# Attention and a rational layer on one core: top bits of early weights on GpSimd, and keys instead of masks

## The chip, the core and the metric

The program runs on one core of one Trainium2 chip, in one launch. The metric is the device time in microseconds from start to end; three runs of a kernel are made and their median stands for it. Times within a run come from one profiled execution.

## What is computed

Queries, keys and values have 4 batches, 8 heads, 768 positions and 64 columns. Each chunk of 32 queries looks at a window of 16 keys to its left, its own 32, 8 to its right, and 8 memory keys. At the ends of a sequence the window is cut. The result goes through a layer with a rational function between two products.

```python
for c in range(nc):                                   # chunks of 32 queries
    l_start, r_end = max(0, c_start - 16), min(S, c_end + 8)
    k_full = np.concatenate([mem_k, k[:, :, l_start:r_end]], axis=2)
    v_full = np.concatenate([mem_v, v[:, :, l_start:r_end]], axis=2)
    scores = scale * np.matmul(q_c, k_full.transpose(0, 1, 3, 2))
    a = np.exp(scores - np.max(scores, axis=-1, keepdims=True))
    a = a / (np.sum(a, axis=-1, keepdims=True) + 1e-09)
    out[:, :, c_start:c_end] = np.matmul(a, v_full)
...
h = x @ w_in                                          # x: 3072 x 512, w_in: 512 x 2048
P = a[0] + a[1] * h + a[2] * h2 + a[3] * h3
Q = 1.0 + np.abs(b[0]) * np.abs(h) + np.abs(b[1]) * h2
return (P / (Q + 1e-6)) @ w_out                       # w_out: 2048 x 512
```

The weights w_in and w_out are 64-bit floats. The kernel gets them as 64-bit integers and makes 32-bit floats of them itself.

## The kernel before

**Tiles.** The 3072 rows are eight blocks of 384. For each block there are four units of attention (two heads each), which fill x of that block, and 16 steps of the layer, one for each 128 columns of w_in: `g1` makes h (12 matmuls, line 462), a chain on ScalarE, GpSimd and VectorE makes the rational function, and `g2` adds to the block's three outputs (9 matmuls, line 477). Both x and the weights are split into a high and a low part for TensorE (x_hi, x_lo, w_hl), so each product is three.

**Attention of a unit.** Scores go to PSUM (line 347). On VectorE a memset puts -1e30 on the scores of absent keys (lines 357 and 359; 307 and 309 for blocks from the fourth on), a reduction finds the maximum (362), a subtraction makes e (365). ScalarE takes the exponential (369), TensorE transposes (384), ScalarE copies (391), TensorE multiplies with v, which has a column of ones for the sum (402); VectorE divides (412 to 415, making xt), TensorE transposes back (425), ScalarE makes x_hi and xf (429, 432), GpSimd or VectorE x_lo (438, 442). A block is one half of a batch's sequence, so each unit has one chunk at an end of the sequence, the left one in even blocks and the right one in odd, and its memset covers the keys that are absent there.

**Weights.** A weight tile j has two halves, "in" and "out", of 128 x 512 words each, 64 bits a word. The order of the 32 halves is i0 o0 i1 o1 i4 i2 i3 o3 and so on. A half passes five steps, which the code's letters name: w (SP issues the load into w_raw), A (`w_abs`: ScalarE brings the high word's exponent to the range of 32 bits, line 172, into a PSUM tile stage), B (`w_bits`: VectorE shifts stage left by 3, line 177, then joins it with the top three bits of the low word, line 178, in place of that low word), H (ScalarE rounds to w_hl, line 185) and L (GpSimd subtracts to get the low part, line 190). The raw buffer is loaded anew when all its steps are done.

**The chain of the layer.** For each step: ScalarE ha and cy (513, 514), GpSimd cy (518), ScalarE ct (523), VectorE ct (527, 528), ScalarE cr by a logarithm and an exponential (532, 533), VectorE 537 to 539, GpSimd ghi and glo (544, 551).

**What sets the order.** The start, up to the 30th step, is a string of such letters written out by hand (SEQ). Every instruction is pinned in that order, and each engine works its own in that order; an instruction that waits holds up all behind it on its engine. A letter issues all its instructions together, whatever the engine. Loads are all issued by SP, in order. Later steps follow a fixed loop.

Of the kernel before, what the change touches and what calls it, by code (L numbers as in the profile page):

```python
# [16 lines left out]
ALU = mybir.AluOpType  # L17
AX = mybir.AxisListType

CHUNK = 32  # L20
LEFT = 16
RIGHT = 8
WIN = LEFT + CHUNK + RIGHT
MEM = 8
NEG = -1e30
F64_REBIAS = 2.0 ** -111
SIGN_STEP = 2.0 ** 32
W_SCALE = 2.0 ** 8
# [29 lines left out]
"""  # L58
QK_SLOTS = {0: [12, 13, 14, 15], 1: [12, 13, 14, 15], 2: [15, 16]}
WHOLE = 13  # L60
LAST = 122
FINAL = """
o g s p i j t r u y  o g s p i j t r u y  g s p i j t r u y o  g s p i j t r u y  g s p i j t r u y o  s p i j t r u y  o o u y o o
# [10 lines left out]
def attn_moe(ctx, tc, qk, vm, w, ab, out):  # L74
    nc = tc.nc
    P = 128
# [5 lines left out]
    NG = TB // P  # L82
    KEYS = P // 2
# [36 lines left out]
    def pin(ins):  # L120
        if pinned[0]:
            tc.keep_in_program_order(ins)
# [7 lines left out]
    conv, raws, split = {}, {}, {}  # L130
# [28 lines left out]
    def words(key):  # L159
        t = half(raws[key[1]], key[0]).rearrange("p (f two) -> p f two", two=2)  # L160
        return t[:, :, 0], t[:, :, 1]
# [6 lines left out]

    def w_abs(key):
        low, high = words(key)  # L170
        f = conv[key] = ps_a.tile([P, DM], F32, name="stage", tag="pa")
        pin(nc.scalar.activation(f, high.bitcast(F32), AF.Prelu, scale=F64_REBIAS, alpha=-SIGN_STEP))

    def w_bits(key):
        low, high = words(key)
        fi = conv.pop(key).bitcast(U32)
        pin(nc.vector.tensor_scalar(fi, fi, 3, None, op0=ALU.logical_shift_left))  # L177
        pin(nc.vector.scalar_tensor_tensor(low, low, 29, fi, op0=ALU.logical_shift_right, op1=ALU.bitwise_or))

# [123 lines left out]
    def pair_max(i, p):  # L303
        u = unit[i, p]
        sv = u.pop("s")
        if i % 2 == 0:
            pin(nc.vector.memset(sv[0:CHUNK, :, 0, 0:LEFT], NEG))
        else:
            pin(nc.vector.memset(sv[P - CHUNK:P, :, NG - 1, KEYS - RIGHT:KEYS], NEG))
        mx = sm.tile([P, 2, NG], F32, name="mx")  # L310
        pin(nc.vector.tensor_reduce(mx, sv, axis=AX.X, op=ALU.max))
        e = u["e"] = at.tile([P, NG, KEYS, 2], F32, name="e", tag="e", bufs=2)
        turned = e.rearrange("x g w h -> x g (w h)").rearrange("x g (b h k) -> x g b h k", b=4, h=2)
        for h in range(2):
            pin(nc.vector.tensor_tensor(turned[:, :, :, h], sv[:, h].rearrange("x g (b k) -> x g b k", b=4),
                                        mx[:, h].unsqueeze(2).unsqueeze(3).broadcast_to([P, NG, 4, KEYS // 4]), op=ALU.subtract))
# [33 lines left out]
    def att_max(i, p):  # L350
# [2 lines left out]
        u = unit[i, p]  # L353
        s = u.pop("s")
        sv = s[:, :NG * 2 * KEYS].rearrange("x (g h w) -> x g h w", g=NG, h=2)
        if i % 2 == 0:
            pin(nc.vector.memset(sv[0:CHUNK, 0, :, 0:LEFT], NEG))
        else:
            pin(nc.vector.memset(sv[P - CHUNK:P, NG - 1, :, KEYS - RIGHT:KEYS], NEG))
        mx = sm.tile([P, NG * 2], F32, name="mx")  # L360
        s3 = s[:, :NG * 2 * KEYS].rearrange("x (n w) -> x n w", w=KEYS)
        pin(nc.vector.tensor_reduce(mx, s3, axis=AX.X, op=ALU.max))
# [191 lines left out]
    done = dict.fromkeys("wABHL", 0)  # L554
# [146 lines left out]
    evac(*order[-1])  # L701


def padded(x, mem):
    x = np.pad(x, ((0, 0), (0, 0), (LEFT, RIGHT), (0, 0)))
    return np.concatenate([x, mem], axis=2)


def spread(first, count, S):
# [8 lines left out]
def lay_out(q, k, v, mem_k, mem_v):  # L718
    B, H, S, D = q.shape
    n = S // CHUNK // 2  # L720
    kp, vp = padded(k, mem_k), padded(v, mem_v)
    spans = [spread(half * n, n, S) for half in range(2)]
    keys = WIN + MEM
    kt = np.stack([kp[:, :, rows] for rows in spans], axis=2)
# [3 lines left out]
    qk = np.stack([np.concatenate([kt[:, :, 0], qt[:, :, 0]], axis=3),  # L728
                   np.concatenate([qt[:, :, 1], kt[:, :, 1]], axis=3)], axis=2)
    qk[BLOCKWISE:, :, 1] = np.concatenate([kt[BLOCKWISE:, :, 1], qt[BLOCKWISE:, :, 1]], axis=3)  # L730
    vw = np.concatenate([vw, np.ones(vw.shape[:4] + (1,), vw.dtype)], axis=4)
    vm = vw.reshape(B, H // 2, 2, 2, n, keys, D + 1).transpose(0, 3, 1, 2, 5, 4, 6)
    vm = np.array(vm.reshape(2 * B, H // 2, 2, keys, n * (D + 1)))
    late = vm[BLOCKWISE:].reshape(2 * B - BLOCKWISE, H // 2, 2, 4, keys // 4, n * (D + 1))
# [20 lines left out]
```

## Time and profile before

| | |
|---|---|
| median of three runs | 619.96 us (619.09 to 620.35) |
| the profiled execution | 619.44 us |
| its span, first to last instruction | 617.6 us |
| TensorE, matmuls | 599.1 us, 97% |
| VectorE | 495.3 us, 80% |
| ScalarE | 435.8 us, 71% |
| GpSimd | 433.0 us, 70% |

The span is what the instructions take; 1.84 us of the profiled execution lie around it. Shares of the whole span hide that the kernel has two parts: a start, in which loads, weights and attention are made ready, and a long row of matmuls. The start has to be read in order of time, engine by engine: a row shows when an instruction began, how long it took and, in brackets, how long the engine stood idle before it and what ended that.

### The profile page before, as it was taken

What the parts mean: (1) busy time and instruction counts of PE and PEld (TensorE: products, weight loads), DVE (VectorE), ACT (ScalarE), POOL (GpSimd) and SP (SyncE); (2) the same over time, 40 slices, a digit from 0 to 9 for tenths busy, and PEclk for the clock granted to TensorE, in tenths of its full rate; (3) what the DMA queues carried; (4) which work ended last, traced back from release to release, by engine and by line L of the source; (5) the groups of instructions that cost most, each with busy time, mean ns of one, the idle gap of its engine ahead of it and who ended that gap; (6) DMA issues with size and microseconds to landing.
All of it is one profiled execution on the core that took longest, in us unless ns stands there. A gap on an engine that the chain in (4) does not pass through costs nothing.

```text
span 617.6 us, 14151 instructions
## 1 busy us (share of the span) xinstructions
PE 599.1 (97%) x5275; PEld 528.8 (86%) x5275; DVE 495.3 (80%) x991; ACT 435.8 (71%) x822; POOL 433.0 (70%) x459
## 2 busy tenths in 40 slices
PE   6689999999999999999999999999999999999997
PEld 5568889899888888988889898888889888989996
DVE  6899998898867979788778787777878777666674
ACT  5799888798756766666667766676676766676674
POOL 2579987879966667766767676766767676776773
PEclk9999999999999999999999999999999999999999
DMA  7989437103023574342221322242122310010001
GB/s 259 359 280 360 162 110 254 48 1 146 2 83 86 177 212 146 119 133 81 82 81 38 116 68 75 81 133 82 36 62 68 101 27 14 14 51 2 0 1 51
DMA packets 42788, 64.81 MB, mean 105 GB/s; under 512 B 25696, under 2 KB 25696, under 8 KB 42336
## 3 DMA queue, kind: packets, MB, share of 16 engines
q1 hardware_dynamic: 41856, 60.61, 30.6%
q10 hardware_dynamic: 576, 1.74, 0.9%
q0 software_dynamic: 288, 1.57, 0.8%
q8 instruction: 41, 0.67, 0.4%
q14 instruction: 27, 0.22, 0.1%
HBM read 46.60 MB, written 9.44 MB: 91 GB/s over the span
## 4 chain that ended last, share of the span: by engine, by line
PE 53%; issue 18%; POOL 15%; DMA 5%; DVE 4%; ACT 2%; SPq 1%; POOLq 0%; DVEq 0%
PE o L477 25%; PE h L462 24%; POOL glo L551 6%; POOL ghi L544 6%; DMA qk<-in_qk_dram 2%; DMA w_raw<-in_w_dram 2%; POOL x_lo L440 1%; PE pairs L300 1%; POOL cy L518 1%; PE pairs L323 1%; SPq L125 1%; DMA v_main<-in_vm_dram 1%; DVE stage L177 1%; PE pa L347 1%; DVE ct L528 1%
## 5 line engine op out<-in xcount | busy, mean ns | idle before, releaser
L462 PE MATMUL h<-x_hi,w_hl 128*128 128x384 f32 x1024 | 265.1, 339 | 0.9 <-DVE ct L528 0.5
L477 PE MATMUL o<-w_hl,ghi 128*128 128x512 f32 x768 | 239.6, 393 | 0.0
L518 POOL TENSOR_TENSOR cy<-cy,ha 128x384 f32<-128x384 f32 x128 | 130.4, 1019 | 140.8 <-ACT cy L514 135.5
L462 PEld LDWEIGHTS h<-x_hi,w_hl 128*128 128x128 f32 x1024 | 185.3, 188 | 12.6 <-DVE ct L528 2.1
L462 PE MATMUL h<-x_lo,w_hl 128*128 128x384 f32 x512 | 172.5, 337 | 0.0
L477 PEld LDWEIGHTS o<-w_hl,ghi 128*128 128x128 f32 x768 | 141.8, 188 | 20.8 <-issue 0.8
L477 PE MATMUL o<-w_hl,glo 128*128 128x512 f32 x384 | 150.9, 393 | 0.0
L551 POOL TENSOR_TENSOR glo<-ct,ghi 128x384 fp32r<-128x384 f32 x127 | 129.1, 1017 | 8.9
L513 ACT ACTIVATE ha<-h 128x384 f32<-128x384 f32 x128 | 62.9, 492 | 91.7 <-PE h L462 89.4
L527 DVE TENSOR_TENSOR ct<-ct,h 128x384 f32<-128x384 f32 x128 | 70.1, 548 | 57.6 <-ACT ct L523 57.4
L544 POOL TENSOR_TENSOR ghi<-ct,zero 128x384 fp32r<-128x384 f32 x127 | 105.4, 830 | 3.8 <-DVE ct L539 2.7
L537 DVE SCALAR_TENSOR_TENSOR ct<-ct,par,cr 128x384 f32<-128x384 f32 x128 | 78.5, 613 | 33.9 <-ACT cr L533 30.9
L532 ACT ACTIVATE cr<-cy 128x384 f32<-128x384 f32 x128 | 63.2, 494 | 58.3 <-POOL cy L518 54.1
L462 PEld LDWEIGHTS h<-x_lo,w_hl 128*128 128x128 f32 x512 | 96.0, 188 | 0.0
L514 ACT ACTIVATE cy<-ha,bab 128x384 f32<-128x384 f32 x128 | 90.9, 710 | 4.5 <-DVE cr L538 0.3
L477 PEld LDWEIGHTS o<-w_hl,glo 128*128 128x128 f32 x384 | 72.0, 187 | 20.2 <-POOL glo L551 0.8
L523 ACT ACTIVATE ct<-h,par 128x384 f32<-128x384 f32 x128 | 84.1, 657 | 0.1
L528 DVE SCALAR_TENSOR_TENSOR ct<-ct,par,h 128x384 f32<-128x384 f32 x128 | 78.7, 615 | 4.5
L539 DVE SCALAR_TENSOR_TENSOR ct<-cr,ct 128x384 f32<-128x384 f32 x128 | 71.4, 558 | 4.4
L538 DVE SCALAR_TENSOR_TENSOR cr<-cy,cr 128x384 f32<-128x384 f32 x128 | 71.1, 556 | 0.4
L533 ACT ACTIVATE cr<-cr 128x384 f32<-128x384 f32 x128 | 60.8, 475 | 4.0
L190 POOL TENSOR_TENSOR w_hl<-w_raw,w_hl 128x512 fp32r<-128x512 f32 x32 | 42.1, 1316 | 6.8 <-ACT w_hl L185 6.1
(69 smaller groups left out, 406.9 us busy)
## 6 DMA issues: line engine op xcount, KB each, us to landing
w_raw<-in_w_dram SPq DMA_DIRECT2D x26, 512.0 KB, 7.0
v_main<-in_vm_dram SPq DMA_DIRECT2D x20, 390.0 KB, 4.7
qk_pairs<-in_qk_dram SPq DMA_DIRECT2D x16, 424.0 KB, 4.2
out_dram<-stage SPq DMA_DIRECT2D x24, 256.0 KB, 3.8
qk<-in_qk_dram SPq DMA_DIRECT2D x24, 212.0 KB, 4.8
v_main<-in_vm_dram SPq DMA_DIRECT2D x20, 195.0 KB, 6.0
eT<-blocks SPq DMA_DIRECT2D x80, 48.0 KB, 2.0
xf<-blocks SPq DMA_DIRECT2D x80, 48.0 KB, 2.0
```

The costliest lines, as they stand in the source:

```text
L462: pin(nc.tensor.matmul(h[:, :TB], lhsT=wt[:, cols], rhs=xt[i][:, ct, :], start=m == 0, stop=m == last))
L477: ins = nc.tensor.matmul(o, lhsT=gt[:, cols], rhs=wt, start=begin and m == 0, stop=end and m == 2)
L514: pin(nc.scalar.activation(c["y"], c["ha"], AF.Identity, scale=B1, bias=B0))
L518: pin(nc.gpsimd.tensor_tensor(c["y"], c["y"], c.pop("ha"), op=ALU.mult))
L523: pin(nc.scalar.activation(c["t"], c["h"], AF.Identity, scale=A3, bias=A2))
L527: pin(nc.vector.tensor_tensor(t, t, h, op=ALU.mult))
L528: pin(nc.vector.scalar_tensor_tensor(t, t, A1, h, op0=ALU.add, op1=ALU.mult))
L537: pin(nc.vector.scalar_tensor_tensor(t, t, A0, r, op0=ALU.add, op1=ALU.mult))
L538: pin(nc.vector.scalar_tensor_tensor(r, yy, QC, r, op0=ALU.add, op1=ALU.mult))
L539: pin(nc.vector.scalar_tensor_tensor(t, r, 2.0, t, op0=ALU.subtract, op1=ALU.mult, reverse0=True))
L544: pin(nc.gpsimd.tensor_tensor(ghi, chain[z]["t"], zero.broadcast_to([P, TB]), op=ALU.add))
L551: pin(engine.tensor_tensor(glo, chain.pop(z)["t"], gh[z].bitcast(F32), op=ALU.subtract))
```

## The change

It has two parts. For the first eight halves of weights, `w_abs` gets an instruction on GpSimd that reads the upper 16 bits of each low word, multiplies by 2 to the power -13, caps at 7 and writes that over the low word: the word's top three bits. VectorE then needs one instruction where it had two: it shifts stage left by 3 and joins it with that word. The other 24 halves stay as they were.

The memsets on scores are gone in all units. Instead, where a key is absent, the host's layout has a copy of the first memory key, and v has a row of zeros there, its column of ones too. The maximum over a row is then the same, and an absent key adds nothing to the sum or to the product.

```diff
+TOP_BITS = 8
...
     def w_abs(key):
         low, high = words(key)
+        if done["A"] < TOP_BITS:
+            tops = half(raws[key[1]], key[0]).bitcast(mybir.dt.uint16).rearrange("p (f four) -> p f four", four=4)[:, :, 1]
+            pin(nc.gpsimd.tensor_scalar(low, tops, 2.0 ** -13, 7.0, op0=ALU.mult, op1=ALU.min))
         f = conv[key] = ps_a.tile([P, DM], F32, name="stage", tag="pa")
         pin(nc.scalar.activation(f, high.bitcast(F32), AF.Prelu, scale=F64_REBIAS, alpha=-SIGN_STEP))
 
     def w_bits(key):
         low, high = words(key)
         fi = conv.pop(key).bitcast(U32)
+        if done["B"] < TOP_BITS:
+            pin(nc.vector.scalar_tensor_tensor(low, fi, 3, low, op0=ALU.logical_shift_left, op1=ALU.bitwise_or))
+            return
         pin(nc.vector.tensor_scalar(fi, fi, 3, None, op0=ALU.logical_shift_left))
         pin(nc.vector.scalar_tensor_tensor(low, low, 29, fi, op0=ALU.logical_shift_right, op1=ALU.bitwise_or))
...
     def pair_max(i, p):
         u = unit[i, p]
         sv = u.pop("s")
-        if i % 2 == 0:
-            pin(nc.vector.memset(sv[0:CHUNK, :, 0, 0:LEFT], NEG))
-        else:
-            pin(nc.vector.memset(sv[P - CHUNK:P, :, NG - 1, KEYS - RIGHT:KEYS], NEG))
...
     def att_max(i, p):
...
-        if i % 2 == 0:
-            pin(nc.vector.memset(sv[0:CHUNK, 0, :, 0:LEFT], NEG))
-        else:
-            pin(nc.vector.memset(sv[P - CHUNK:P, NG - 1, :, KEYS - RIGHT:KEYS], NEG))
...
-def padded(x, mem):
-    x = np.pad(x, ((0, 0), (0, 0), (LEFT, RIGHT), (0, 0)))
-    return np.concatenate([x, mem], axis=2)
+def padded(x, mem, pad):
+    return np.concatenate([np.repeat(pad, LEFT, axis=2), x, np.repeat(pad, RIGHT, axis=2), mem], axis=2)
...
-    kp, vp = padded(k, mem_k), padded(v, mem_v)
+    v1, mem_v1 = (np.concatenate([x, np.ones(x.shape[:3] + (1,), x.dtype)], axis=3) for x in (v, mem_v))
+    kp, vp = padded(k, mem_k, mem_k[:, :, :1]), padded(v1, mem_v1, np.zeros_like(v1[:, :, :1]))
...
-    vw = np.concatenate([vw, np.ones(vw.shape[:4] + (1,), vw.dtype)], axis=4)
```

GpSimd's queue, before the change, from the low part of i1 to the low parts of i2 and i3. The numbers at a name tell buffers apart: w_raw_282 holds tile 1, w_raw_378 tile 4, w_raw_413 tile 2 and w_raw_418 tile 3.

```order
L438 TENSOR_TENSOR x_lo0_104<-xf_468,x_hi0_102 128x384
L438 TENSOR_TENSOR x_lo0_104<-xf_494,x_hi0_102 128x384
L190 TENSOR_TENSOR w_hl_411<-w_raw_282,w_hl_411 128x512
L190 TENSOR_TENSOR w_hl_540<-w_raw_378,w_hl_540 128x512
L518 TENSOR_TENSOR cy_592<-cy_592,ha_593 128x384
L190 TENSOR_TENSOR w_hl_608<-w_raw_413,w_hl_608 128x512
L190 TENSOR_TENSOR w_hl_644<-w_raw_418,w_hl_644 128x512
```

The same place after the change, where w_raw_279 holds tile 1, w_raw_373 tile 4, w_raw_409 tile 2 and w_raw_413 tile 3:

```order
L196 TENSOR_TENSOR w_hl_407<-w_raw_279,w_hl_407 128x512
L173 TENSOR_SCALAR w_raw_373<-w_raw_373 128x512
L436 TENSOR_TENSOR x_lo0_104<-xf_462,x_hi0_102 128x384
L436 TENSOR_TENSOR x_lo0_104<-xf_488,x_hi0_102 128x384
L173 TENSOR_SCALAR w_raw_409<-w_raw_409 128x512
L196 TENSOR_TENSOR w_hl_407<-w_raw_279,w_hl_407 128x512
L196 TENSOR_TENSOR w_hl_534<-w_raw_373,w_hl_534 128x512
L173 TENSOR_SCALAR w_raw_413<-w_raw_413 128x512 x2
L516 TENSOR_TENSOR cy_586<-cy_586,ha_587 128x384
```

The conversion of i4 now stands ahead of two x_lo, that of i2 ahead of the low parts of o1 and i4, and those of i3 and o3 between these and the first cy of the layer's chain.

VectorE's queue, before the change, from the join of i2 to the chain's first steps; stage_499, stage_555 and stage_600 belong to i2, i3 and o3:

```order
L177 TENSOR_SCALAR stage_499<-stage_499 128x512
L178 SCALAR_TENSOR_TENSOR w_raw_413<-w_raw_413,stage_499 128x512
L177 TENSOR_SCALAR stage_555<-stage_555 128x512
L178 SCALAR_TENSOR_TENSOR w_raw_418<-w_raw_418,stage_555 128x512
L359 MEMSET pa_527 32x2x8
L362 TENSOR_REDUCE mx_603<-pa_527 128x6
L365 TENSOR_TENSOR e_605<-pa_527,mx_603 128x3x2x64
L527 TENSOR_TENSOR ct_596<-ct_596,h_507 128x384
L528 SCALAR_TENSOR_TENSOR ct_596<-ct_596,par_96,h_507 128x384
L177 TENSOR_SCALAR stage_600<-stage_600 128x512
L178 SCALAR_TENSOR_TENSOR w_raw_418<-w_raw_418,stage_600 128x512
L537 SCALAR_TENSOR_TENSOR ct_596<-ct_596,par_96,cr_610 128x384
```

The same place after the change, where stage_494, stage_550 and stage_594 belong to i2, i3 and o3:

```order
L181 SCALAR_TENSOR_TENSOR w_raw_409<-stage_494,w_raw_409 128x512
L181 SCALAR_TENSOR_TENSOR w_raw_413<-stage_550,w_raw_413 128x512
L360 TENSOR_REDUCE mx_596<-pa_521 128x6
L363 TENSOR_TENSOR e_598<-pa_521,mx_596 128x3x2x64
L525 TENSOR_TENSOR ct_590<-ct_590,h_501 128x384
L526 SCALAR_TENSOR_TENSOR ct_590<-ct_590,par_96,h_501 128x384
L181 SCALAR_TENSOR_TENSOR w_raw_413<-stage_594,w_raw_413 128x512
L535 SCALAR_TENSOR_TENSOR ct_590<-ct_590,par_96,cr_603 128x384
```

Three shifts and a memset are gone. The joins now read what GpSimd wrote, and the reduction stands right behind the join of i3.

## Rows read from the trace of the kernel before

**Rows 1.** The page, part 1: busy us and share of the span.
```profile
PE 599.1 (97%) x5275; PEld 528.8 (86%) x5275; DVE 495.3 (80%) x991; ACT 435.8 (71%) x822; POOL 433.0 (70%) x459
```

**Rows 2.** Busy time by stretch: length, then the engines, clock, DMA share, GB/s.
```profile
0.00:30.00 30.00, 19.52 (x343) 15.08 (x343) 22.36 (x51) 18.68 (x37) 12.71 (x22) 1.00 0.88 306
30.00:50.00 20.00, 17.52 (x193) 14.24 (x193) 18.49 (x37) 18.88 (x39) 14.53 (x15) 1.00 0.88 296
50.00:100.00 50.00, 49.21 (x368) 41.70 (x367) 48.25 (x93) 45.04 (x87) 44.20 (x44) 1.00 0.54 194
100.00:600.00 500.00, 499.15 (x4316) 446.57 (x4315) 397.40 (x797) 344.62 (x646) 353.64 (x373) 1.00 0.26 78
```

**Rows 3.** Groups by shape, GpSimd's, then VectorE's: busy us, mean ns | idle before.
```profile
L518 POOL TENSOR_TENSOR cy<-cy,ha 128x384 f32<-128x384 f32 x128 | 130.4, 1019 | 140.8 <-ACT cy L514 135.5 <-DVE xt L336 4.2 <-DMA v_main<-in_vm_dram 0.8
...
L190 POOL TENSOR_TENSOR w_hl<-w_raw,w_hl 128x512 fp32r<-128x512 f32 x32 | 42.1, 1316 | 6.8 <-ACT w_hl L185 6.1 <-DVE ct L527 0.6
...
L217 POOL MEMSET qk<- 128x464 f32 x5 | 2.3, 485 | 0.0
...
masks.py:199 POOL TENSOR_SCALAR_AFFINE_SELECT ident<-ident 128x128 f32<-128x128 f32 x1 | 0.3, 294 | 0.0
...
L747 POOL MEMSET const-float32-1.0<- 128x1 f32 x1 | 0.1, 99 | 0.0
...
L527 DVE TENSOR_TENSOR ct<-ct,h 128x384 f32<-128x384 f32 x128 | 70.1, 548 | 57.6 <-ACT ct L523 57.4
```

**Rows 4.** TensorE in order of time, 32 to 43 us: start, us [idle before].
```profile
32.35 0.86 PE L347 MATMUL pa<-qk 128*32 128x128 f32 x24 [0.97 <-DMA qk<-in_qk_dram]
...
37.80 0.55 PE L384 MATMUL pa<-ident,e 128*128 128x128 f32 x3
...
40.10 0.34 PE L462 MATMUL h<-x_lo,w_hl 128*128 128x384 f32 x1
41.32 0.52 PE L425 MATMUL pa<-ident,xt 128*128 128x128 f32 x3 [0.88 <-DVE xt L415]
42.34 0.62 PE L462 MATMUL h<-x_hi,w_hl 128*128 128x384 f32 x2 [0.50 <-DVE ct L528]
```

**Rows 5.** ScalarE in order of time, 26 to 38 us.
```profile
26.84 0.62 ACT L172 ACTIVATE stage<-w_raw 128x512 f32<-128x512 f32 x1 [2.25 <-DMA w_raw<-in_w_dram]
...
29.88 0.65 ACT L172 ACTIVATE stage<-w_raw 128x512 f32<-128x512 f32 x1 [0.65 <-DMA w_raw<-in_w_dram]
...
35.13 0.49 ACT L532 ACTIVATE cr<-cy 128x384 f32<-128x384 f32 x1
...
37.17 0.51 ACT L369 ACTIVATE e<-e 128x384 f32<-128x384 f32 x1
```

**Rows 6.** GpSimd in order of time, 23 to 34 us.
```profile
23.72 1.31 POOL L190 TENSOR_TENSOR w_hl<-w_raw,w_hl 128x512 fp32r<-128x512 f32 x1
24.98 1.00 POOL L438 TENSOR_TENSOR x_lo<-xf,x_hi 128x384 fp32r<-128x384 f32 x1
28.32 1.01 POOL L438 TENSOR_TENSOR x_lo<-xf,x_hi 128x384 fp32r<-128x384 f32 x1 [2.34 <-ACT xf L432]
...
33.65 1.02 POOL L518 TENSOR_TENSOR cy<-cy,ha 128x384 f32<-128x384 f32 x1 [0.79 <-DMA v_main<-in_vm_dram]
```

**Rows 7.** VectorE in order of time, 33 to 40 us.
```profile
33.64 0.56 DVE L362 TENSOR_REDUCE mx<-pa 128x6 f32<-128x384 f32 x1
...
35.94 0.70 DVE L177 TENSOR_SCALAR stage<-stage 128x512 uint32<-128x512 uint32 x1
36.67 0.69 DVE L178 SCALAR_TENSOR_TENSOR w_raw<-w_raw,stage 128x512 uint32<-128x512 uint32 x1
...
38.94 0.09 DVE L357 MEMSET pa<- 32x32 f32 x1
39.06 0.56 DVE L362 TENSOR_REDUCE mx<-pa 128x6 f32<-128x384 f32 x1
```

**Rows 8.** The chain of waits up to 100 us: start, us, what.
```profile
69.88 0.09 DVE pa L357
```

More of the change, by code (lines that the diff above doesn't have):

```diff
@@ L24 @@
 MEM = 8
-NEG = -1e30
 F64_REBIAS = 2.0 ** -111
```

## The prediction

> **What bounds the kernel now.** I read the busy shares first, then the same shares by stretches. TensorE is busy for 599.1 us of a span of 617.6 us [rows 1]. In the stretches the reader is to see where it is not: it idles 10.5 us of the first 30, 2.5 us from 30 to 50, 0.8 us from 50 to 100, and 0.85 us in the next 500 [rows 2]. From 50 us on the kernel is a row of matmuls with no holes, and nothing that VectorE or GpSimd saves there can shorten it by more than those 1.6 us. So the change, which works on the first 40 us and takes memsets out elsewhere, is worth what it does to the moment at which the dense row begins.
>
> In the first 30 us the loads are the limit: DMA is busy 0.88 of that time [rows 2], ScalarE stands still 2.25 us until weights land at 26.84 us [rows 5], and TensorE waits 0.97 us for queries and keys as late as 32.35 us [rows 4]. VectorE's work up to there waits for the same loads. The first stall of TensorE that a compute engine makes is the one at 41.32 us: the third product of the first layer ended at 40.44 us (40.10 plus 0.34), and the transposes behind it wait 0.88 us for VectorE's xt. Behind them the next product waits 0.50 us for VectorE's ct [rows 4]. VectorE is busy 18.5 of the 20 us from 30 to 50 [rows 2]; it is the engine to relieve, and the place is 32 to 41 us.
>
> **What is removed.** Eight shifts of line 177 leave VectorE, 0.70 us each; from one start to the next such a shift takes 0.73 us (35.94 to 36.67) [rows 7]. Four belong to weights that the loads hold back (up to 27 us) and are worth nothing, since TensorE and ScalarE wait for loads there. The fifth and sixth stand ahead of 33.64 us and the eighth at 35.94 us. Of the memsets on scores, 32 in all, each takes 0.12 us from its start to that of the reduction behind it (38.94 to 39.06) [rows 7]. One lies between 34 and 41 us on VectorE's way to xt; two more (69.88 us and 76.06 us, of which the row of the first is shown) lie on the chain of waits that leads to the last holes before 100 us [rows 8]. These two are worth 0.24 us. The 20 memsets of the later blocks lie under the dense matmuls: nothing, and if that cover were gone, 20 x 0.12 = 2.4 us.
>
> The copies of a key and the zero rows in v change what the arrays hold, not their shapes: every load stays as it is, and this costs nothing.
>
> **What is added.** Eight tensor_scalar on GpSimd, 128x512, reading 16-bit integers and writing 32-bit ones. Call the price of one d. No such row is in the trace, so I bound it. Below: a memset of 464 words takes 0.485 us [rows 3], and with the 0.1 us that a memset of one column takes, 0.53 us for 512. Above: the subtraction of line 190, 128x512 with two inputs, one of them the same spaced-out low words, takes 1.316 us [rows 3]. A second way to the upper end: for the same product of two 128x384 inputs GpSimd takes 1.019 us and VectorE 0.548 us, a ratio of 1.86 [rows 3]; VectorE's shift at 0.70 us [rows 7] times that is 1.30 us. The row nearest in kind is the select that makes the identity, with one input and some arithmetic: 0.294 us for 128 columns. Without the same 0.1 us it holds some 0.19 us for 128 columns, or 0.78 us for 512, and 0.88 us with the 0.1 us [rows 3]. I take d = 0.9 and keep 0.53 and 1.3 for the range. Nothing in the rows excludes more than 1.3, since no GpSimd row here converts between integers and floats.
>
> The Trainium skill ("GPSIMD Engine Reference", sections 3 and 4.1) speaks against the move: elementwise work belongs on VectorE, and GpSimd is about twice as slow with two inputs; the 1.86 above agrees [rows 3]. The same table says that one input runs at roughly line rate, and section 7 gives some 1.9 cycles an element while the step is at most 8 bytes, which is the step here; at the page's 1.2 GHz that makes an estimate of 0.81 us. By the first rule (twice 0.70 us) the sum below would be +1.8 us, by the second 0.0. No row here decides between them.
>
> **What is moved: GpSimd's queue from 26.84 us.** The new instruction stands in program order at the place of the Prelu on ScalarE, so it waits for its load, and all that is queued behind it on GpSimd waits too. Earlier, the first pair of w_hl stands behind a conversion as well, and SP's next load of raw weights behind that pair; with DMA 0.88 busy [rows 2] the loads already queued cover that. Before, the queue had time: it stood idle for 2.34 us until 28.32 us, and reached cy at 33.65 us [rows 6]. Now, with the loads where they are (i4 at 26.84 us, i2 at 29.88 us, by ScalarE's starts [rows 5]):
> - i4 runs 26.84 to 26.84+d; two x_lo of 1.01 us follow, until 28.86+d. The first product needs them. With d = 0.9 the second ends at 29.76 us, 0.43 us later than before (28.32 plus 1.01). Even if the product feels all of it, the wait of 0.97 us for a load that stands behind it at 32.35 us covers it [rows 4]; past 0.97 us (d of 1.4) it would count.
> - i2 starts at 29.88 us as long as d is at most 1.02. Then come two w_hl, 1.26 us from start to start [rows 6]: 32.40+d.
> - i3 and o3: cy starts at 32.40+3d = 35.10 us, against 33.65 us.
>
> Two engines wait for that. **ScalarE:** cr needs cy, which ends at 33.42+3d = 36.12 us; it began at 35.13 us, so +0.99 us. Behind it in ScalarE's queue stands the exponential of 37.17 us, and behind that TensorE's transposes at 37.80 us [rows 4, 5]: the third product ends at 41.43 us. Of that delay 0.88 us is the old wait for xt; only what goes past 41.32 us counts, here 0.11 us. **VectorE:** the combine of i3 can start when i3's bits are there, 32.40+2d = 34.20 us, and takes 0.69 us. The reduction behind it, at 33.64 us before, starts at 34.89 us: +1.25 us. Then the eighth shift is gone (-0.73) and one memset (-0.12): xt is +0.40 us, and TensorE's transposes stand at 41.72 us. This is later than 41.43 us, so it decides: TensorE +0.40 us. The wait of 0.50 us at 42.34 us is for the ct two steps behind xt on the same engine and moves with it.
>
> **Sum.** +0.40 at 42 us, -0.24 from the two memsets later: +0.16 us. As a rule of d: 2d - 1.64 us through VectorE, 3d - 2.83 us through ScalarE, the larger counts, and beyond d = 1.02 each gains another d - 1.02. At d = 0.53 this is -0.6 us, at 0.82 zero, at 1.3 +1.35 us. So the relief of VectorE is spent on waiting for GpSimd. The profiled execution took 619.44 us and would take 619.6 us; it lies 0.5 us below the median of the runs, 619.96 us, which becomes 620.1 us. A measurement of this kernel tells a change from none at about 0.2%, 1.24 us.
>
> **Rivals.**
> - *GpSimd becomes the bound of the start (slower).* Place: cy behind four conversions, then cr and the exponential behind it on ScalarE. With d above 1.02 the sum is 4d - 3.85, and it passes 1.24 us from d = 1.27 on. At the two-input price of 1.3 us it is +1.35 us, 621.3 us; at 1.6 us, if the conversions come on top, +2.55 us, 622.5 us. For it: the 1.86 ratio, and the conversions that no row shows. Against it: one input only, and the select's row. By the Trainium skill's rule of twice the time (same page, section 3) the sum would fall here. Chance 0.25.
> - *VectorE's relief arrives (faster).* If GpSimd is never late, TensorE's 0.88 us at 41.32 us goes, and with it the 0.8 us of holes from 50 to 100 us: -1.7 us, 618.3 us. For it: VectorE is 92% busy there and loses 2.3 us of work. Against it: 2d - 1.40 reaches -0.88 only at d = 0.26, half the price of a memset. Chance 0.10.
> - *Forecast: the two cancel within the bound,* d from 0.4 to 1.27. Chance 0.65.
>
> **How the numbers follow.** Predicted is the forecast, 620.1 us. The range takes the lower end of d (-0.6 us) with the scatter of the runs (some 0.6 us about their median): 618.8 us; above, the rival at d of some 1.5 us: +2.2 us, 622.2 us. About one in ten is left out on either side. Faster 0.10, same 0.65, slower 0.25.
>
> **What the profile will show.** GpSimd's new group of eight rows with its mean, d: this decides everything. If I am right, cy of the first chain starts near 35 us, ScalarE's first cr near 36 us, and TensorE's wait for xt ends near 41.7 us; VectorE shows new idle time ahead of the combines, released by GpSimd. TensorE's idle time from 100 us on stays under 1 us. I am wrong if d is far from 0.9, if a load lands at another time because the raw weights are given back later, or if TensorE's idle time after 50 us changes by more than its 1.6 us.

## The result: slower by one per cent, and the profile after

| | before | after |
|---|---|---|
| median of four runs each, on one chip | 620.15 us (619.09 to 620.4) | 626.37 us (625.62 to 626.92) |
| after over before, 95% interval | | 1.0103 (1.0085 to 1.012) |
| profiled execution, its span | 619.44 us, 617.6 us | 626.09 us, 624.3 us |

The forecast was 620.1 us, in a range from 618.8 to 622.2 us. The kernel came out 6.2 us slower by the medians (6.4 us by the ratio), 4 us past the upper end. The likeliest case (no change) did not happen; the rival "GpSimd becomes the bound of the start" did, beyond the price it was given. The ratios here and below leave out two executions far off all others, one of keys_only (3305.73 us) and one of before beside one_op (2051.03 us).

First the page's busy line of after, then the busy time by stretch (start and end, length, five engines, granted clock as a share, DMA share, GB/s). Before's are [rows 1, 2].

```profile
PE 603.5 (97%) x5275; PEld 532.7 (85%) x5275; DVE 484.7 (78%) x951; ACT 435.6 (70%) x822; POOL 448.7 (72%) x467
```

```profile
0.00:30.00 30.00, 21.10 (x334) 16.24 (x334) 16.47 (x35) 17.66 (x34) 19.49 (x24) 0.94 0.89 295
30.00:50.00 20.00, 13.12 (x127) 11.35 (x128) 11.53 (x24) 13.57 (x28) 17.48 (x15) 0.83 0.75 254
50.00:100.00 50.00, 49.53 (x410) 41.60 (x409) 47.83 (x93) 45.34 (x88) 46.89 (x46) 1.00 0.58 199
100.00:600.00 500.00, 499.40 (x4311) 446.02 (x4310) 395.03 (x778) 345.43 (x648) 352.08 (x372) 1.00 0.27 80
```

VectorE has 40 instructions fewer and 10.6 us less to do, GpSimd 8 more and 15.7 us more. The loss shows between 30 and 50 us: TensorE idles 6.9 us there, before 2.5, and its granted clock is 0.83 of full, before 1.00. From 50 us on the row of matmuls is as dense as it was, so what is lost by 50 us stays lost.

Next is the price that the prediction called d, among GpSimd's groups by shape (busy us, mean ns of one, idle time before).

```profile
L173 POOL TENSOR_SCALAR w_raw<-w_raw 128x512 uint32<-128x512 uint16 x8 | 16.0, 2004 | 9.7 <-DMA w_raw<-in_w_dram 9.2
```

d is 2.0 us; I had taken 0.9 and kept 0.53 to 1.3 for the range. GpSimd in order of time shows what the last six of the eight do (start, duration; in brackets the idle time before and what ended it; before's are [rows 6]).

```profile
19.44 1.98 POOL L173 TENSOR_SCALAR w_raw<-w_raw 128x512 uint32<-128x512 uint16 x1 [1.64 <-DMA w_raw<-in_w_dram]
21.50 2.57 POOL L196 TENSOR_TENSOR w_hl<-w_raw,w_hl 128x512 fp32r<-128x512 f32 x2
24.15 2.03 POOL L173 TENSOR_SCALAR w_raw<-w_raw 128x512 uint32<-128x512 uint16 x1
26.26 1.00 POOL L436 TENSOR_TENSOR x_lo<-xf,x_hi 128x384 fp32r<-128x384 f32 x1
27.23 1.29 POOL L196 TENSOR_TENSOR w_hl<-w_raw,w_hl 128x512 fp32r<-128x512 f32 x1
28.60 2.03 POOL L173 TENSOR_SCALAR w_raw<-w_raw 128x512 uint32<-128x512 uint16 x1
30.71 1.99 POOL L436 TENSOR_TENSOR x_lo<-xf,x_hi 128x384 fp32r<-128x384 f32 x2
32.78 1.99 POOL L173 TENSOR_SCALAR w_raw<-w_raw 128x512 uint32<-128x512 uint16 x1
34.85 2.60 POOL L196 TENSOR_TENSOR w_hl<-w_raw,w_hl 128x512 fp32r<-128x512 f32 x2
37.53 4.05 POOL L173 TENSOR_SCALAR w_raw<-w_raw 128x512 uint32<-128x512 uint16 x2
41.67 1.00 POOL L516 TENSOR_TENSOR cy<-cy,ha 128x384 f32<-128x384 f32 x1
```

From 19.44 us to the first cy there is not one wait in brackets: each row starts when the one before is done, with 0.08 us on either side of a conversion. The first cy starts at 41.67 us, before at 33.65 [rows 6], 8.0 us later. Who waits for it is the pair that the prediction named, ScalarE's cr and behind it the exponential, and on TensorE the transposes (before: [rows 5], [rows 4]):

```profile
26.89 0.63 ACT L175 ACTIVATE stage<-w_raw 128x512 f32<-128x512 f32 x1 [1.00 <-DMA w_raw<-in_w_dram]
...
42.70 0.49 ACT L530 ACTIVATE cr<-cy 128x384 f32<-128x384 f32 x1 [5.96 <-POOL cy L516]
...
44.74 0.51 ACT L367 ACTIVATE e<-e 128x384 f32<-128x384 f32 x1
```

```profile
40.29 0.87 PE L400 MATMUL pa<-v_main,eT 128*32 128x130 f32 x24 [1.87 <-DVE w_raw L181]
45.30 0.90 PE L382 MATMUL pa<-ident,e 128*128 128x128 f32 x3 [4.14 <-ACT e L367]
45.85 0.99 PE L460 MATMUL h<-x_hi,w_hl 128*128 128x384 f32 x2
46.64 0.52 PE L460 MATMUL h<-x_lo,w_hl 128*128 128x384 f32 x1
...
48.91 0.34 PE L460 MATMUL h<-x_lo,w_hl 128*128 128x384 f32 x1
49.09 0.49 PE L423 MATMUL pa<-ident,xt 128*128 128x128 f32 x3
49.33 0.60 PE L460 MATMUL h<-x_hi,w_hl 128*128 128x384 f32 x2
```

The transposes stand at 45.30 us instead of 37.80: 7.5 us, as much as cr and the exponential are late by (7.57 us each). Two things then happen that the sum did not have. The third product takes 3.40 us (45.85 to 48.91 plus 0.34), where it took 2.34 before (38.10 to 40.44), 1.06 us more: its first single matmul takes 0.52 us, its last 0.34. And the old waits behind it are gone: the transposes at 49.09 us follow at once (0.88 us given back), and the next product at 49.33 us does not wait for ct (0.50 us given back, which I had left standing). It starts 7.0 us later than before (49.33 against 42.34 us [rows 4]), and the span ends 6.7 us later.

### The profile page after: what moved, and what is told of

It reads as the page before. It is cut to its first block, busy times and chain, and to the rows that moved or that the text cites. A ratio compares the mean times of both kernels' runs of the same rounds, so it can differ in the third digit from the quotient of the medians.

```text
span 624.3 us, 14117 instructions
## 1 busy us (share of the span) xinstructions
PE 603.5 (97%) x5275; PEld 532.7 (85%) x5275; DVE 484.7 (78%) x951; ACT 435.6 (70%) x822; POOL 448.7 (72%) x467
## 4 chain that ended last, share of the span: by engine, by line
PE 45%; issue 22%; POOL 22%; DMA 4%; ACT 2%; DVE 2%; SPq 1%; POOLq 0%
PE h L460 21%; PE o L475 21%; POOL glo L549 8%; POOL ghi L542 8%; DMA w_raw<-in_w_dram 3%; POOL x_lo L438 2%; POOL cy L516 2%; SPq L125 1%; POOL w_hl L196 1%; PE pairs L306 1%; PE pairs L325 1%; POOL w_raw L173 1%; PE pa L400 1%; DMA out_dram<-stage 1%; DMA qk<-in_qk_dram 0%
## 5 line engine op out<-in xcount | busy, mean ns | idle before, releaser
L535 DVE SCALAR_TENSOR_TENSOR ct<-ct,par,cr 128x384 f32<-128x384 f32 x128 | 78.5, 613 | 38.9 <-ACT cr L531 37.8
```

The source lines that it names most:

```text
L535: pin(nc.vector.scalar_tensor_tensor(t, t, A0, r, op0=ALU.add, op1=ALU.mult))
```

## The experiments

Each kernel was timed beside the kernel before on the same chip. A difference in us below is the ratio less one, times the median of before in that comparison; after is +6.4 us by that measure, and the expectations write the 6.2 us of the medians. The kernel price ran once and is used for its rows alone.

**What GpSimd asks for a tensor_scalar (price).** The kernel before with nine of them on scratch data, one after the other in the start.

```diff
+        for to, fro, s1, s2, o1, o2 in [
+                (flat(dst)[:, :512], flat(src)[:, :512], 2.0, 7.0, ALU.mult, ALU.min),
+                (lo.bitcast(U32), w16, 2.0 ** -13, 7.0, ALU.mult, ALU.min),
+                (lo, hi, 2.0, 7.0, ALU.mult, ALU.min),
...
+                (lo, hi, 2.0, None, ALU.mult, None)]:
+            pin(nc.gpsimd.tensor_scalar(to, fro, s1, s2, op0=o1, **({} if o2 is None else dict(op1=o2))))
```

> The kernel before, with nine tensor_scalar of 128x512 on a scratch buffer added to GpSimd's idle time after its memsets (5 to 17 us); their result is not used. It measures the price by itself: 32-bit floats packed and with gaps, 16-bit integers to 32-bit integers with gaps (the form of the change), the same packed, floats to integers, integers to floats, 32-bit integers to 32-bit integers, and two forms with one operation instead of two. Theory 'type': the 2.0 us of the change come from converting integers, so floats to floats take 0.8 to 1.0 us and every form with an integer takes more, about half of the extra each for reading and for writing. Theory 'gaps': the 2.0 us come from the spaced-out words, so floats with gaps take about 2 us too and packed integers about 1 us. Theory 'two operations': the forms with one operation take about half.

Seven of the nine, each by itself (duration min/median/max of the one, start, shape). The rows at 5.8 us and 12.0 us have packed operands, the others spaced-out ones; those at 16.1 and 22.0 us do one operation, the others two.

```profile
L629 POOL TENSOR_SCALAR price<-price x1: 1928/1928/1928, 5.8 to 5.8; 128x512 f32<-128x512 f32 x1
...
L629 POOL TENSOR_SCALAR price<-price x1: 1982/1982/1982, 7.9 to 7.9; 128x512 uint32<-128x512 uint16 x1
...
L629 POOL TENSOR_SCALAR price<-price x1: 2032/2032/2032, 9.9 to 9.9; 128x512 f32<-128x512 f32 x1
...
L629 POOL TENSOR_SCALAR price<-price x1: 1919/1919/1919, 12.0 to 12.0; 128x512 uint32<-128x512 uint16 x1
...
L629 POOL TENSOR_SCALAR price<-price x1: 1614/1614/1614, 16.1 to 16.1; 128x512 uint32<-128x512 uint16 x1
...
L629 POOL TENSOR_SCALAR price<-price x1: 2007/2007/2007, 19.9 to 19.9; 128x512 uint32<-128x512 uint32 x1
...
L629 POOL TENSOR_SCALAR price<-price x1: 1606/1606/1606, 22.0 to 22.0; 128x512 f32<-128x512 f32 x1
```

All three explanations put up there fall. The type is worth nothing (1.982 us for the change's 16 to 32 bits, 2.032 us for floats in the same layout), gaps between the words 0.06 to 0.10 us, and the second operation 0.37 to 0.43 us, a fifth and not half. Nor is it VectorE's company: in after the conversion of i3 takes 1.98 us from 37.53 us, while VectorE stands idle (4.05 us, until 39.54 us). What is left is the instruction itself: 1.6 us for 512 columns with a single multiplication, more than the 1.316 us of a subtraction of two tensors of that shape [rows 3]. Why it is so no run here shows.

**The forecast at the price it assumed (stand_in).** In place of the conversion GpSimd adds zero to zero and writes the low word: the same place, the same waits, another price. The three bits from the low word are then zero.

```diff
-            pin(nc.gpsimd.tensor_scalar(low, tops, 2.0 ** -13, 7.0, op0=ALU.mult, op1=ALU.min))
+            pin(nc.gpsimd.tensor_tensor(low.bitcast(F32), zero.broadcast_to([P, DM]), zero.broadcast_to([P, DM]), op=ALU.add))
```

> The changed kernel with another GpSimd instruction in the conversion's place, on the same words, behind the same load and with the same readers: an addition of two constants broadcast over 128x512, which writes zeros over the low words, so the lowest three bits of these weights' fractions are dropped. Line 544 has this operation with one broadcast input at 0.83 us for 384 columns, so d should be some 1.1 us. It asks whether the prediction's rule of d holds at the price that was assumed: by the rule +0.2 to +0.9 us on the kernel before, first cy at 35.7 us. Rival 'any instruction there costs' (the wait for the load in GpSimd's queue or the pairing of engines costs, not the price): 3 us slower or more.

Measured: 619.4 us, ratio 0.9995 (0.9986 to 1.0005), -0.3 us. The group of its eight instructions, then its first cy:

```profile
L172 POOL TENSOR_TENSOR w_raw<-zero 128x512 f32<-128x512 f32 x8 | 8.3, 1040 | 9.5 <-DMA w_raw<-in_w_dram 9.5
```

```profile
34.54 1.01 POOL L515 TENSOR_TENSOR cy<-cy,ha 128x384 f32<-128x384 f32 x1
```

At 1.04 us the rule of the prediction (through VectorE, 2d - 1.64 plus d - 1.02) gives +0.5 us and a first cy at 35.5 us; measured are -0.3 us (by the interval from -0.9 to +0.3) and 34.5 us. ScalarE can work on i4's load 0.9 us earlier in this profile (25.97 us against the 26.84 us of [rows 5]), which is most of the difference in cy. So eight instructions in the same places, on the same words and behind the same loads, cost nothing that shows as long as they are cheap: it is the price, not their being there.

**Which half of the change (tops_only, keys_only).** tops_only keeps the memsets and the layout of before; keys_only makes no conversions.

```diff
-TOP_BITS = 8
+TOP_BITS = 0
```

> Only the first part of the change: eight conversions on GpSimd; the memsets and the layout of keys are those of the kernel before. Theory 'queue': 6.3 to 7.3 us slower than the kernel before, that is the whole loss and the few tenths that the missing memsets give back; cy of the first chain starts near 41.7 us instead of 33.65. Rival 'keys': clearly less than 6 us slower.

> Only the second part of the change: no memsets on scores, absent keys are copies of a key; no half of weights is converted on GpSimd. Theory 'queue' (GpSimd's conversions hold up cy, and with it everything): all of the loss is in the other part, and this one is 0.2 to 0.6 us faster than the kernel before, from the memsets between 33 and 76 us. Rival 'keys': the memsets or the copies have a part in the loss, and this one is slower than the kernel before by 1 us or more.

Measured: tops_only 626.67 us, ratio 1.011 (1.009 to 1.0131), +6.8 us; keys_only 619.34 us, ratio 0.9992 (0.998 to 1.0004), -0.5 us. The whole loss is the conversions'. The memsets with their key copies are worth -0.5 us (by the interval from -1.2 to +0.2), against the -0.24 us of the prediction; no run separates the two.

**Which four (tops4, late4).** tops4 converts i0, o0, i1 and o1 on GpSimd, late4 the other four, i4, i2, i3 and o3.

```diff
-TOP_BITS = 8
+TOP_BITS = 4
```

```diff
-        if done["A"] < TOP_BITS:
+        if 4 <= done["A"] < TOP_BITS:
...
-        if done["B"] < TOP_BITS:
+        if 4 <= done["B"] < TOP_BITS:
```

> The changed kernel with GpSimd's conversions for the first four halves only (i0, o0, i1, o1); the other four go as in the kernel before. Theory 'queue': GpSimd falls behind from the third conversion on (19.4 us), but without the later ones it has caught up when cy of the first chain comes, near 33 to 34 us, so nearly nothing is lost: between 0.6 us faster and 0.6 us slower than the kernel before. Rival 'each its share' (eight conversions cost the same, 0.8 us each): 2.6 us slower, half of the loss less the memsets' gain.

> The changed kernel with GpSimd's conversions for the second four halves only (i4, i2, i3, o3). GpSimd's queue is free until 26.84 us, as the prediction had it. Theory 'queue': with d = 2.0 the prediction's rule gives cy at 39.4 us and +4.2 us; with TensorE's slower clock behind the longer wait up to 0.9 us more: 4.0 to 5.3 us slower than the kernel before. What is missing to the 6.2 us of the changed kernel is the queue that was late already at 26.84 us. Rival 'each its share': 2.6 us slower.

Measured: tops4 619.77 us, ratio 1.0005 (0.9996 to 1.0014), +0.3 us; late4 623.49 us, ratio 1.0068 (1.0052 to 1.0084), +4.2 us. GpSimd in tops4, the first cy; then the product behind xt on TensorE, first in tops4, then in keys_only; then GpSimd and TensorE in late4:

```profile
35.08 1.02 POOL L516 TENSOR_TENSOR cy<-cy,ha 128x384 f32<-128x384 f32 x1 [2.02 <-ACT cy L512]
```

```profile
42.95 0.61 PE L460 MATMUL h<-x_hi,w_hl 128*128 128x384 f32 x2 [0.50 <-DVE ct L526]
```

```profile
41.38 0.61 PE L460 MATMUL h<-x_hi,w_hl 128*128 128x384 f32 x2 [0.50 <-DVE ct L526]
```

```profile
26.08 2.01 POOL L173 TENSOR_SCALAR w_raw<-w_raw 128x512 uint32<-128x512 uint16 x1 [1.39 <-DMA w_raw<-in_w_dram]
28.17 1.99 POOL L436 TENSOR_TENSOR x_lo<-xf,x_hi 128x384 fp32r<-128x384 f32 x2
30.25 2.01 POOL L173 TENSOR_SCALAR w_raw<-w_raw 128x512 uint32<-128x512 uint16 x1
32.33 2.60 POOL L196 TENSOR_TENSOR w_hl<-w_raw,w_hl 128x512 fp32r<-128x512 f32 x2
35.02 4.06 POOL L173 TENSOR_SCALAR w_raw<-w_raw 128x512 uint32<-128x512 uint16 x2
39.16 1.00 POOL L516 TENSOR_TENSOR cy<-cy,ha 128x384 f32<-128x384 f32 x1
```

```profile
42.80 0.90 PE L382 MATMUL pa<-ident,e 128*128 128x128 f32 x3 [4.15 <-ACT e L367]
```

The early four alone cost nothing that shows against the kernel before (-0.2 to +0.9 us): GpSimd has time for them, and its queue still stands idle 2.02 us ahead of cy. But they are not free. They take another way: VectorE's join of o1 waits for GpSimd until 25.29 us (before it started at 22.70 us) and holds up the maximum and e behind it, so that the first product starts at 30.22 us instead of 29.02 and ScalarE's cy comes late. The product behind xt starts at 42.95 us, before at 42.34 [rows 4], and at 41.38 us in keys_only, which makes no conversions; by the medians tops4 is 0.8 us slower than keys_only, though their intervals overlap.

The late four alone are the case that the prediction worked out, a queue free when i4 lands. At d = 2.0 its rule gives a first cy at 32.40 + 3d + (d - 1.02) = 39.4 us, transposes at 43.1 us and a sum of +4.15 us; measured are 39.16 us, 42.80 us and +4.2 us (by the interval +3.2 to +5.2). That the three agree so closely is in part that small things cancel: i4's load is 0.8 us early here (26.02 us on ScalarE), against it stand 0.08 us on either side of each conversion and a slower TensorE, of which more below. The change costs another 2.2 us (6.4 less 4.2). By the medians some 0.8 us of them is what tops4 loses to keys_only, and 1.4 us appear only when early and late conversions come together; that is within the scatter of these comparisons, so it is the trace that shows how they meet: the early ones make the queue late for the late ones. In late4 i4's conversion starts at 26.08 us, when its load is there; in after at 28.60 us, while ScalarE works on the same load from 26.89 us on.

**Does TensorE's clock take its share (filled)?** After, with the product with v of one unit made five times instead of once, which puts matmuls into TensorE's wait of 4.1 us.

```diff
-            pieces[kind](i, p)
+            for _ in range(FILL if token == "d11" else 1):
+                pieces[kind](i, p)
```

> The changed kernel with the 12 small products of one attention unit made five times instead of once, in TensorE's wait of 4.1 us ahead of 45.3 us; the result is the same numbers. It keeps TensorE busy there and leaves GpSimd's queue alone. Theory 'clock' (a part of the loss is that TensorE's granted clock is 0.5 from 41.3 to 48 us, behind its waits, so that the third product takes 3.2 instead of 2.3 us): 0.5 to 0.9 us faster than the changed kernel, 5.3 to 5.7 us slower than the one before, with a granted clock of 1.0 at 45.8 us. Rival 'no clock' (the third product's end is covered by the wait for xt behind it): within 0.2 us of the changed kernel.

Measured: 625.16 us, ratio 1.0089 (1.0075 to 1.0103). TensorE in filled, then the stretches 43 to 46 and 46 to 48 us, first of after, then of filled (the sixth number behind the length is the granted clock):

```profile
40.27 3.54 PE L403 MATMUL pa<-v_main,eT 128*32 128x130 f32 x120
45.19 0.55 PE L383 MATMUL pa<-ident,e 128*128 128x128 f32 x3 [1.39 <-ACT e L368]
45.49 0.60 PE L463 MATMUL h<-x_hi,w_hl 128*128 128x384 f32 x2
```

```profile
43.00:46.00 3.00, 0.70 (x4) 0.70 (x4) 2.13 (x5) 2.94 (x7) 1.04 (x2) 0.50 0.85 263
46.00:48.00 2.00, 2.00 (x8) 2.00 (x8) 1.90 (x6) 1.97 (x6) 2.00 (x2) 0.50 0.87 282
```

```profile
43.00:46.00 3.00, 1.61 (x38) 1.34 (x27) 2.24 (x5) 2.93 (x8) 1.05 (x2) 1.00 0.27 72
46.00:48.00 2.00, 2.00 (x14) 1.88 (x12) 1.90 (x6) 1.97 (x6) 2.00 (x2) 1.00 0.93 291
```

In after the clock stands at its lower level (0.50, 1.2 GHz) behind a wait of 4.1 us and TensorE does 8 matmuls from 46 to 48 us; with the wait filled down to 1.4 us it stays at 2.4 GHz and does 14, and the third product takes 2.34 us again (45.49 to 47.49 plus 0.34). The trace shows plainly that the product is slow at the lower clock and fast again at the full one. What that is worth in the end, 0.9 us (6.4 less 5.5), is less sure: the two intervals overlap, and in the trace the transposes for xt start 1.4 us earlier (47.67 us), but the product behind them, which now waits 0.42 us for ScalarE, only 0.75 us (48.58 against 49.33 us). Nor does the length of a wait alone tell the clock: in filled the first product, behind a wait of 0.84 us, runs at 0.50 from 30.3 us on.

**Less of the price (one_op).** After, with a multiplication alone in the conversion, which the first experiment prices at 1.6 us. The three bits are rounded otherwise.

```diff
-            pin(nc.gpsimd.tensor_scalar(low, tops, 2.0 ** -13, 7.0, op0=ALU.mult, op1=ALU.min))
+            pin(nc.gpsimd.tensor_scalar(low, tops, 7.49 / 65535, None, op0=ALU.mult))
```

> The kernel after with one arithmetic operation less in each of GpSimd's eight conversions (a multiplication alone, without the minimum), so the same number of instructions on the same operands at about 1.61 us in place of 2.0 (from the cost run). The three bits that reach the low words are rounded otherwise; nothing else changes. Theory 'queue and clock': GpSimd is busy without a gap from 19.44 us in the kernel after, and six conversions stand between there and the first cy, so that cy moves by 6 x 0.39 = 2.3 us, from 41.67 to about 39.3, and the sum from +6.2 to about +3.9 over the kernel before; TensorE's wait shrinks from 4.1 to about 1.8 us, and if the granted clock then stays full over the third first-layer product, 0.7 us more comes back: +3.0 to +4.1 in all. Rival 'rule on record': four conversions ahead of the first cy, 4d less 3.85, plus the constant 2.4 us that the kernel after lies above that rule: 4 x 0.39 = 1.6 us back, +4.6. Rival 'not the price': the conversions are late because of their loads or because of VectorE, and their price does not matter: +6.2 unchanged.

Measured: 622.98 us, ratio 1.0056 (1.0039 to 1.0072), +3.5 us. Its group, the conversion of i4 and the first cy on GpSimd, TensorE's wait, and the clock:

```profile
L173 POOL TENSOR_SCALAR w_raw<-w_raw 128x512 uint32<-128x512 uint16 x8 | 12.8, 1601 | 8.7 <-DMA w_raw<-in_w_dram 8.2
```

```profile
26.52 1.56 POOL L173 TENSOR_SCALAR w_raw<-w_raw 128x512 uint32<-128x512 uint16 x1
...
37.94 1.00 POOL L516 TENSOR_TENSOR cy<-cy,ha 128x384 f32<-128x384 f32 x1
```

```profile
41.58 0.90 PE L382 MATMUL pa<-ident,e 128*128 128x128 f32 x3 [3.73 <-ACT e L367]
```

```profile
43.00:46.00 3.00, 3.00 (x11) 3.00 (x10) 2.85 (x6) 2.68 (x7) 3.00 (x4) 0.50 0.94 261
```

0.4 us off each conversion gives back 2.9 us (6.4 less 3.5): by the medians seven times the price's change, not the four times that the rule of the prediction has. The rival without any effect of the price (+6.2 us) falls. The one with the rule's slope (+4.6 us) lies just outside the interval (+2.4 to +4.5 us), but it is counted from the kernel after, which has an interval of its own (+5.3 to +7.4 us), so it is not excluded. The sum is the one that the theory of queue and clock gave (+3.0 to +4.1 us). But two of its steps missed. The first cy starts at 37.94 us, not 39.3, and TensorE's wait stays long (3.73 us, not 1.8), because the work ahead of it came earlier as well. cy is where the rule has it for a free queue (32.40 + 4 x 1.60 - 1.02 = 37.8 us): the conversion of i4 began at 26.52 us, 0.7 us behind ScalarE's start on the same load (25.82 us), but ahead of the 26.84 us that the rule counts from. In what lies above the rule's 2.55 us is the clock, 0.50 here too: the third product takes 4.18 us (42.13 to 45.79 plus 0.52), 1.84 us more than before, of which the wait for ct, gone here too, gives 0.50 us back. Part of the earlier queue is the load of i1, which ScalarE could work on at 17.97 us here and at 19.39 us in the profile of after. Over all the profiles of this study it was between 17.7 and 19.4 us, before's own at 18.99. Within one execution such a shift moves the queue's lateness by as much, and I cannot take it out of a single profile.

**Without GpSimd, and with little of it (shift_only, tops2).** shift_only makes no conversions, and VectorE only shifts stage; the three bits are left out. tops2 converts i0 and o0 alone and leaves no bits out.

```diff
-        if done["B"] < TOP_BITS:
-            pin(nc.vector.scalar_tensor_tensor(low, fi, 3, low, op0=ALU.logical_shift_left, op1=ALU.bitwise_or))
-            return
...
+            pin(nc.vector.tensor_scalar(low, fi, 3, None, op0=ALU.logical_shift_left))
```

```diff
-TOP_BITS = 8
+TOP_BITS = 2
```

> The changed kernel without GpSimd's conversions: for the first eight halves VectorE only shifts, so the lowest three bits of these weights' fractions are dropped, and GpSimd's queue is that of the kernel before. It shows what VectorE's relief is worth where it costs nothing. By the prediction's terms TensorE's wait of 0.88 us for xt goes and 0.24 us later: 0.9 to 1.7 us faster than the kernel before, first cy at 33.65 us. Rival 'relief is worth nothing' (loads and ScalarE hold the start anyway): no more than keys_only gives, 0.2 to 0.6 us faster.

> The kernel after with GpSimd's conversions for the first two halves alone (i0 and o0, which start near 4.9 and 14.5 us in the kernel after, where GpSimd otherwise waits for loads); the other six low words are made by VectorE in two steps, as in the kernel before. It is the version that the runs so far point to. Theory 'queue': these two conversions stand in GpSimd's idle time, so nothing behind them is late, the first cy starts no later than in the kernel before (33.65 us), and what is left is the relief of VectorE by two steps and the key copies: 0 to -1 us, between the run with the key copies alone (-0.5) and the run with shifts alone (-1.2). Rival 'any conversion costs': a quarter of +6.2 us, +1.5 us. Rival 'loads': the first low words are bounded by the loads, so that two conversions change nothing against the key copies alone: -0.5 us, within what can be told from the theory only by the trace (the cy before 33 us for the theory, at 33.65 for this rival).

Measured: shift_only 618.61 us, ratio 0.998 (0.9967 to 0.9993), -1.2 us; tops2 618.54 us, ratio 0.998 (0.9967 to 0.9992), -1.2 us. TensorE's wait for xt, 0.88 us before [rows 4], is not there in shift_only, and in tops2 it is:

```profile
40.38 0.52 PE L423 MATMUL pa<-ident,xt 128*128 128x128 f32 x3 [0.28 <-DVE xt L413]
```

shift_only is the rival "VectorE's relief arrives" made real, priced at -1.7 us: all the shifts' relief and no wait for GpSimd. Its interval (-2.0 to -0.4 us) holds that price, and also the upper part of what the rival "relief is worth nothing" allowed (-0.2 to -0.6 us). tops2 is by its median the fastest of the kernels here that leave nothing out, faster than before (by 0.5 to 2.0 us) and than after. That two conversions cost nothing is shown (+1.5 us would be the quarter of the loss), but not that they bring anything over the key copies alone: its wait for xt (0.28 us) is like that of keys_only (0.19 us), its first cy, at 33.32 us, lies between the two expectations, and the intervals overlap.

## Why the prediction was wrong, point by point

**The price of one conversion: the step that failed.** "I take d = 0.9 and keep 0.53 and 1.3 for the range", from the select's row and, above, the subtraction of two tensors. d is 2.0 us. Both ends were taken from other operations in the belief that fewer inputs cost less on GpSimd; the first experiment shows the opposite for this operation, 1.6 us with one input against 1.3 us with two [rows 3]. The sentence "Nothing in the rows excludes more than 1.3" named the hole, and the range should have followed it. The reason I gave for that hole, the conversion of types, was wrong as well: types cost nothing here. Of the two rules of the Trainium skill ("GPSIMD Engine Reference") the trace agrees with neither. Section 4.1 has one input at roughly line rate, and section 7 led to an estimate of 0.81 us, which is less than half of what the row shows. Twice VectorE's time (section 3) came nearer, but VectorE's 0.70 us [rows 7] stand against 2.0 us, a ratio of 2.9 (2.3 against the 1.61 us of one operation, as VectorE's shift has).

**The rule for d: right where it was made for.** With the queue free at i4's landing the rule's cy, transposes and sum are those of late4 to some 0.3 us, and those of stand_in to 1 us. At d = 2.0 it gives +4.15 us. The place, cy behind four conversions and then cr and the exponential on ScalarE, was the rival's, and it is the way the delay takes. Which engine decides is by the rule also a matter of d: VectorE up to 1.19, ScalarE's chain beyond. That VectorE decides at 0.9, as I wrote, no run shows; in stand_in, at 1.04, it is already ScalarE's chain: TensorE waits 1.30 us for the exponential ahead of 38.19 us and not for xt at 40.84 us. Two slips in the working changed nothing: "4d - 3.85" holds from 1.19 on, not from 1.02, and of the band "d from 0.4 to 1.27" the lower end gives -0.84 us by the rule, not the bound of 1.24 us.

**The queue, taken as free at 26.84 us: the second step that failed.** "Before, the queue had time" was true of before [rows 6] and was carried over to after. But two conversions (i1 and o1), three low parts and an x_lo come ahead of i4 between 19.44 and 28.60 us with no wait between them, so i4's conversion starts 1.76 us past the 26.84 us that I counted from. With d = 0.9 the two conversions would have been 1.1 us shorter each, i4's turn would have come at 26.4 us, and the step would have held: in stand_in, at 1.04 us, i4's instruction starts at 26.02 us after a wait for its load of 0.54 us. SP, too, issues the two raw loads that stand behind the first pair of w_hl only at 24.09 us, when that pair ends (21.50 + 2.57), before at 22.54 us; in that the cover I named held, since no wait for a load shows on GpSimd from 19.44 us on. Together with the 0.08 us on either side of a conversion, some 0.5 us in all, this accounts for cy: 39.38 + 1.76 + 0.5 = 41.6, measured 41.67 us. That early and late conversions together cost some 2 us more than the late ones is shown by after and late4, whose intervals do not meet; how much of the 1.76 us comes from the later load of i1 in the profile of after stays open.

**The early four: put at nothing.** The sum has no term for the conversions of i0, o0, i1 and o1; they were to lie under the loads. tops4 shows that they also hold up VectorE's joins and with them the first product. In after this first product is 1.9 us late as well (30.89 against 29.02 us), but the wait of 4.1 us behind it hides that.

**TensorE's clock: not in the sum.** A wait of 4.1 us on TensorE was never in my table, since at d = 0.9 there is none. Behind it the granted clock is 0.50, the third product takes 1.06 us more, and from the transposes ahead of it to its start it is 0.55 us where it was 0.30. In filled both are gone, though only 0.75 us of it reaches the next product. Between 20 and 25 us the mean clock is also low in after (0.66), but in keys_only as well (0.67), which is not slower.

**What is given back.** I took off 0.88 us for the old wait for xt and let the 0.50 us of ct stand ("moves with it"). It went too: VectorE had made ct at 48.53 us, ahead of TensorE at 49.33. So the rule's +4.15 us without the 0.24 us of later memsets (+4.39), 1.76 us of queue, 0.5 us of gaps and 1.06 + 0.25 us of clock make +8.0 us at the transposes for xt (measured 49.09 against 41.32 us: +7.8). Less the ct wait (0.50 us) and 0.28 us of faster transposes that is +7.2 us at the product that follows (measured +7.0).

**Right:** the dense row hands a delay on nearly unchanged (7.0 us at 49.33 us, 6.7 us at the end); the memsets and the copies of a key together are worth some tenths (keys_only, -1.2 to +0.2 us). VectorE's new idle time stands where I said, released by GpSimd:

```profile
39.54 0.69 DVE L181 SCALAR_TENSOR_TENSOR w_raw<-stage,w_raw 128x512 uint32<-128x512 uint32 x1 [4.05 <-POOL w_raw L173]
```

And what was to decide, decided: "I am wrong if d is far from 0.9".

## What to carry to other kernels

When work moves to an engine and the trace has no row of that operation there, the rows of other operations do not bound its price: leave the upper end open, work out from which price on the sum turns over, and let the chances follow the distance to it. Count the queue of the engine that takes the work from the first moved instruction on, at the upper price too, since a queue with slack at one price has none at twice that. And place moved work where the engine waits for something else anyway: two conversions in GpSimd's idle time cost nothing that shows, eight cost 6 us.

## What the runs showed of the hardware

- GpSimd's tensor_scalar with two operations takes 1.92 to 2.04 us for 128x512, and 1.6 us with one; types and gaps between words change that by 0.1 us at most (price, after, one_op). An addition of a column spread over that size takes 1.04 us (stand_in), a subtraction of two tensors 1.32 us [rows 3].
- After a wait of 3.7 to 4.2 us TensorE's granted clock is 0.50 (after, late4, one_op), and matmuls that take 0.34 us take 0.52 us. Behind a wait of 1.4 us, with matmuls ahead of it, it is 1.00 (filled at 45.2 us). But it is 0.50 also behind 0.84 us (filled at 30.4 us) and 1.21 us (tops4 at 29.7 us).
- The load of i1, issued between 11.98 and 12.13 us in each of these kernels, let ScalarE begin between 17.7 and 19.4 us, at times that differ from profile to profile.
